# Attention and a squared-ReLU MLP on one core: a third chunk by plain products, and a planner that costs the DMA traffic

## The chip, the cores and the metric

One core of a Trainium2 chip. The metric is the device time of one execution in microseconds (us): the median of 3 runs was 941.05 us (940.84, 941.05 and 945.44). The profile is of one more execution.

## The reference

```python
def _attn_ref(q, k, v):                      # q, k, v: 8 x 8 x 576 x 64
    scores = scale * np.matmul(q, k.transpose(0, 1, 3, 2))
    bias = slopes[:, None, None] * (-np.abs(rel))[None, :, :]
    mask = (rel >= 0) & (rel < 128)
    scores = np.where(mask, scores + bias[None], -1000000000.0)
    attn = np.exp(scores - np.max(scores, axis=-1, keepdims=True))
    attn = attn / (np.sum(attn, axis=-1, keepdims=True) + 1e-09)
    return np.matmul(attn, v)

def _moe_ref(x, w_in, w_out):                # x: 4608 x 512, d_ff 2048
    h = np.maximum(x @ w_in, 0.0)
    return h * h @ w_out

x = attn_out.transpose(0, 2, 1, 3).reshape(4608, 512)
out = _moe_ref(x, w_in, w_out)
```

## The kernel before

The 4608 tokens are nine chunks of 512 (numbered 0 to 8), and d_ff is 16 blocks f of 128. Everything is fp32: each operand of the MLP is split into a high and a low part of a faster type, and each product of blocks is three matmuls (high-high, high-low, low-high).

**The MLP.** The first product of a chunk, x @ w_in, is made in one of two ways. Chunks 0 and 1 take it directly (`gemm1`, line 287): a block f is 12 matmuls of 512 columns; ScalarE then takes the ReLU (line 301), VectorE squares (304), ScalarE rounds the high part (310) and VectorE subtracts for the low part (312). Chunks 2 to 8 take Strassen's scheme: two blocks f are one unit u (8 units in a chunk), and a unit is seven products of 6 matmuls with 256 columns (`product`, line 363) where the plain way needs 24 matmuls of 512 columns. The products read seven forms of x (B11, T1, B21, B22, T2, T3, T4, made once a chunk by `Couple.out`, line 659) and, for four of the seven, sums of weights. Those sums are computed once (`add_weights`, line 343), written to DRAM, and read again for every unit (`load_sum`, line 358; five buffers in turn). `combine` (line 387) adds the products up on VectorE: u1 needs product 6, u3 needs product 5 and u1, c22 needs product 7 and u3; products 2, 3 and 4 go into the banks that s1, u3 and c22 have read, so they wait for these three. The second product (`second`, line 321) adds 12 matmuls of 512 columns for each f, in four steps m of 3; it runs some 8 steps behind. After the 16th f the four sums go out (`copy_out`, line 331, `send_out`, 337): m = 0 and 2 are copied by VectorE, m = 1 and 3 by ScalarE, into two tiles of two halves each; `copy_out` takes a new tile when m is even and otherwise uses the last one taken.

**Attention.** A couple is 512 tokens of a pair of heads; 36 couples in all, four a chunk, each made well before its chunk is due. A *visit* on TensorE (`visit`, line 684) multiplies the weights of the old couple by its values and makes the scores of the new couple. Behind it runs a chain: bias and minimum on VectorE (454), exp on ScalarE (461), sums and reciprocals on VectorE (473, 474), the multiplication by the reciprocals on GpSimd (485), a transpose by blocks on VectorE (533), four writes each of two halves to DRAM (538) and two reads back in another order (543). The next visit needs both reads. A visit comes every two units.

**The order of the work.** Every engine's order is written out. `Line` (line 965) takes steps with an engine, a cost in us, what they come after, and for TensorE the time that its own order gives; due times run backwards from there (`run`), and each engine takes the ready step that is due first. `HANDS` adds 1.5 us after a DMA issue and 0.25 us after TensorE; a read-back is taken as 0.45 us of issue and 2.5 us of landing, whatever else the DMA engines carry. `rest` (line 1033) builds the steps: visits in the direct chunk 1 stand behind the f's of `FIRSTS`, later ones behind every even unit; the sums of weights are all due in chunk 1 (`SUM0` to `SUM3`); the seven products go in the order 1 5 6 7 2 3 4.

## Time and profile before

| | before |
|---|---|
| median of 3 runs | 941.05 us |
| the profiled execution, own time | 940.9 us |
| its span in the profile | 939.1 us |
| mean granted clock of TensorE | 0.987 |
| TensorE busy | 878.9 us (94%) |
| VectorE, ScalarE, GpSimd busy | 680.4, 397.6, 132.6 us |
| DMA | 184.23 MB, 196 GB/s on average |

TensorE's share counts matmuls that overlap one another as busy, so a busy share of 94% does not say that 6% is all there is to gain: what a matmul takes when nothing is late has to be read from stretches in which nothing waits. "Idle before" is time in which an engine stood still, with what ended it. The granted clock is 1.0 at full speed (2.4 GHz) and 0.5 at the lower level (1.2 GHz).

### The profile page before, as it was taken

What the parts mean: (1) busy time and instruction counts of PE and PEld (TensorE: products, weight loads), DVE (VectorE), ACT (ScalarE), POOL (GpSimd) and SP (SyncE); (2) the same over time, 40 slices, a digit from 0 to 9 for tenths busy, and PEclk for the clock granted to TensorE, in tenths of its full rate; (3) what the DMA queues carried; (4) which work ended last, traced back from release to release, by engine and by line L of the source; (5) the groups of instructions that cost most, each with busy time, mean ns of one, the idle gap of its engine ahead of it and who ended that gap; (6) DMA issues with size and microseconds to landing.
All of it is one profiled execution on the core that took longest, in us unless ns stands there. A gap on an engine that the chain in (4) does not pass through costs nothing.

```text
span 939.1 us, 20863 instructions
## 1 busy us (share of the span) xinstructions
PE 878.9 (94%) x7788; PEld 790.8 (84%) x7792; DVE 680.4 (72%) x1952; ACT 397.6 (42%) x1096; POOL 132.6 (14%) x154
## 2 busy tenths in 40 slices
PE   9999999989888999998999998999989999999998
PEld 5788888777788888888888897999888988999997
DVE  7999858998666877776777776677667867755453
ACT  7898754445322433333433342344433343322211
POOL 4322011111011111111011111111111111100000
PEclk9999999999999999999999999999999999999999
DMA  9995454667676647666777677666656776654331
GB/s 347 379 363 160 134 177 138 237 209 236 191 204 177 178 131 243 197 187 175 228 208 203 184 209 220 176 208 198 188 185 195 213 226 188 176 173 147 99 115 46
DMA packets 123909, 184.23 MB, mean 196 GB/s; under 512 B 11808, under 2 KB 55072, under 8 KB 122784
## 3 DMA queue, kind: packets, MB, share of 16 engines
q1 hardware_dynamic: 123376, 182.30, 63.5%
q8 instruction: 62, 1.02, 0.4%
q10 hardware_dynamic: 432, 0.59, 0.2%
q14 instruction: 39, 0.32, 0.1%
HBM read 143.46 MB, written 39.39 MB: 195 GB/s over the span
## 4 chain that ended last, share of the span: by engine, by line
PE 46%; DMA 25%; DVE 16%; ACT 5%; SPq 4%; issue 4%; DVEq 0%; ACTq 0%; POOLq 0%
PE acc L327 21%; DMA pp<-way 14%; PE g L382 7%; PE s L382 5%; DMA way<-pp 4%; PE s L692 4%; SPq L538 3%; PE g L702 3%; PE g L295 3%; DVE pp L533 2%; DMA raw<-in_dram 2%; DMA sum<-sums 2%; DMA out_dram<-o 2%; ACT t L461 2%; DVE r L389 2%
## 5 line engine op out<-in xcount | busy, mean ns | idle before, releaser
L327 PE MATMUL acc<-h,w 128*128 128x512 f32 x1728 | 405.3, 382 | 0.0
L327 PEld LDWEIGHTS acc<-h,w 128*128 128x128 f32 x1728 | 329.1, 197 | 33.4 <-issue 4.6
L485 POOL TENSOR_TENSOR t<-t,nm 128x768 f32<-128x768 f32 x57 | 92.0, 1615 | 193.2 <-DVE nm L474 116.5
L461 ACT ACTIVATE t<-t,nm 128x192 f32<-128x192 f32 x256 | 113.9, 447 | 10.8 <-DVE nm L454 10.7
L454 DVE CUSTOM_DVE_ANT_0 t<-g,cst 128x192 f32<-128x192 f32 (+4 forms) x192 | 53.1, 312 | 87.3 <-PE g L702 85.7
L414 DVE TENSOR_TENSOR h<-r,h 128x512 fp32r<-128x512 f32 x112 | 79.7, 717 | 46.0 <-ACT h L411 44.9
L411 ACT CAST h<-r 128x512 fp32r<-128x512 f32 x112 | 68.5, 617 | 97.4 <-PE acc L327 48.5
L295 PE MATMUL g<-x,w 128*128 128x512 f32 x384 | 89.7, 383 | 6.8 <-ACT r L301 3.0
L382 PEld LDWEIGHTS g<-B,w 128*128 128x128 f32 x672 | 90.0, 191 | 5.6 <-ACT r L301 1.0
L382 PE MATMUL g<-B,w 128*128 128x256 f32 x672 | 93.6, 275 | 0.6 <-ACT r L301 0.6
L692 PE MATMUL s<-pp,v 64*64 64x64 f32 (+1 forms) x1648 | 63.4, 261 | 32.6 <-DMA pp<-way 29.9
L295 PEld LDWEIGHTS g<-x,w 128*128 128x128 f32 x384 | 71.2, 189 | 21.0 <-issue 5.8
L692 PEld LDWEIGHTS s<-pp,v 64*64 64x64 f32 x1648 | 47.7, 143 | 45.8 <-DMA pp<-way 29.3
L382 PE MATMUL s<-T,sum 128*128 128x256 f32 x672 | 84.1, 275 | 0.0
L382 PEld LDWEIGHTS s<-T,sum 128*128 128x128 f32 x672 | 81.6, 192 | 1.2
L406 DVE SCALAR_TENSOR_TENSOR r<-r 128x512 f32<-128x512 f32 x112 | 77.0, 692 | 6.9
L399 ACT ACTIVATE r<-g 128x256 f32<-128x256 f32 x56 | 21.5, 385 | 127.3 <-PE g L382 127.3
L433 POOL MEMSET t<- 64x256 f32 (+1 forms) x56 | 14.2, 253 | 402.3 <-PE g L702 375.8
L389 DVE TENSOR_TENSOR r<-g,u 128x256 f32<-128x256 f32 x112 | 47.3, 422 | 22.7 <-PE g L382 20.7
L382 PE MATMUL g<-B,sum 128*128 128x256 f32 x336 | 50.1, 285 | 12.9 <-DVE r L389 12.9
L533 DVE STREAM_TRANSPOSE pp<-t 128x768 f32<-128x768 f32 x64 | 60.8, 964 | 0.2
L382 PEld LDWEIGHTS g<-B,sum 128*128 128x128 f32 x336 | 41.8, 191 | 19.4 <-DVE r L389 19.4
(108 smaller groups left out, 1118.4 us busy)
## 6 DMA issues: line engine op xcount, KB each, us to landing
sum<-sums SPq DMA_DIRECT2D x224, 256.0 KB, 4.6
pp<-way SPq DMA_DIRECT2D x64, 512.0 KB, 5.6
way<-pp SPq DMA_DIRECT2D x256, 80.0 KB, 2.0
raw<-in_dram SPq DMA_DIRECT2D x32, 512.0 KB, 7.9
qk<-in_dram SPq DMA_DIRECT2D x32, 320.0 KB, 3.1
v<-in_dram SPq DMA_DIRECT2D x32, 320.0 KB, 4.0
qk<-in_dram SPq DMA_DIRECT2D x36, 256.0 KB, 4.0
out_dram<-o SPq DMA_DIRECT2D x35, 256.0 KB, 2.4
```

Of the source, the lines that this page charges most:

```text
L295: nc.tensor.matmul(g, w, in_turn(xs[cc][:, part]), start=i == 0, stop=i == 11)
L327: self.nc.tensor.matmul(self.acc[m], w, in_turn(h), start=(f == 0 and i == 0), stop=(f == NF - 1 and i == 2))
L382: nc.tensor.matmul(to, w, in_turn(t[:, part]), start=i == 0 and k in (1, 5, 6, 7), stop=i == 5, skip_group_check=True,)
L389: V, add = nc.vector, lambda to, a, b: nc.vector.tensor_tensor(to, a, b, op=ALU.add)
L406: V.scalar_tensor_tensor(r, r, 0.0, r, op0=ALU.max, op1=ALU.mult)
L411: nc.scalar.copy(both[:, 0], r)
L414: V.tensor_tensor(hl, r, hh.bitcast(F32), op=ALU.subtract)
L454: self.nc.vector.tensor_tensor_reduce(self.t[r, m, a:e], spot, table[r, a:e], -0.125, least, ALU.add, ALU.min, to,)
L461: e = self.nc.scalar.activation(self.t[:, m], self.t[:, m], AF.Exp, bias=nm[:, m : m + 1], scale=-1.0, accum_out=nm[:, 4 + m : 5 + m],)
L485: self.nc.gpsimd.tensor_tensor(self.t, self.t, rec.unsqueeze(2).to_broadcast([128, 4, 192]), op=ALU.mult)
L533: nc.vector.transpose(squares.rearrange("p b m c -> p m b c"), self.t.rearrange("p m (b c) -> p m b c", c=32))
L692: made.append(mm(to, w, x, start=first and n < 2, stop=not first, skip_group_check=True))
```

## The change

It makes chunk 2 directly, so that three chunks are direct and six go by Strassen's scheme (`NDIR = 3`). The visits behind direct f's become eight (`FIRSTS`), and the sums of weights become due over the two direct chunks 1 and 2. In direct chunks after the first, ScalarE squares. For the third chunk a couple's output is split into two parts (`high`, `low`) where it was seven forms. The order of the seven products is 1 5 6 2 7 3 4, with steps of the second product among them in odd units. Four score matmuls of the new couple (`ahead`) are issued in front of the visit, without a wait for the read-back. `copy_out` takes its tile by m. The planner has one lag for each engine, the DMA transfers of all kinds in turn on one "wire" of 225 KB a us, 1.5 us to spare on read-backs, and steps that share the port of VectorE and GpSimd kept apart.

```diff
+NDIR = 3
+LAGS = {"DVE": 0.13, "Activation": 0.12, "Pool": 0.17, "PE": 0.05}
+WIRE = 225.0
+SPARE = {"rl": 1.5}
+ORDER = ((1, 5, 6, 2, 7, 3, 4), (1, 5, "g", "g", 6, 2, 7, "g", 3, "g", 4))
-FIRSTS = (18, 22, 25, 29)
+FIRSTS = (18, 22, 26, 29, 33, 37, 41, 45)
...
-        if c or f in SQUARES:
+        if c == 0 and f in SQUARES:
...
     def copy_out(self, c, m):
-        if m % 2 == 0:
-            self.both = self.op.tile()
-        self.out_tile[c, m] = self.both[:, m % 2]
+        self.out_tile[c, m] = self.op.all[m // 2][:, m % 2]
...
+def ahead(K, old, new):
+    old.S = K.sc.tile([128, 2, 512], F32, name="s")
+    new.front(old.S, [pool.tile([128, 512], F32, name="g") for pool in (K.low, K.big)])
+    scores(K, new, (0, 0, 0, 1))
...
+    def send(self, name, us, kb, after, do, land, lag):
+        self.add(name, "SP", us, after, do, lag=0.0)
+        self.add(land, "wire", kb / WIRE, [name], None, lag=lag)
...
-                d = min(d, due[n] - TIGHT * us - self.hand(name, self.steps[n][0]))
+                same = s.engine == "PE" and self.steps[n].engine == "PE"
+                d = min(d, due[n] - s.us - (0.0 if same else s.lag) - SPARE.get(name[0], 0.0))
...
-            L.add(("rd", k), "SP", 0.45, [("wl", k), ("wr", 2 * w), ("wr", 2 * w + 1)], step)
-            L.add(("rl", k), f"way{k}", 2.5, [("rd", k)])
+            L.send(("rd", k), 0.4, 512, [("wl", k), ("wr", 2 * w), ("wr", 2 * w + 1)], step, ("rl", k), 1.3)
...
+        if new:
+            first = ("A", v)
+            L.pe(first, 0.3, [*loaded, *banks], do(ahead, K, old, new))
...
+        if c < NDIR:
+            L.add(("x", v, "high"), "Activation", 0.5, [here], do(C.out, "high"))
+            L.add(("x", v, "low"), "DVE", 0.61, [("x", v, "high")], do(C.out, "low"))
...
-            due = L.time + SUM2 + SUM3 * u
-            L.add(("sm", u, i), engine, us, [chain, *after, *more], step, due)
+            L.add(("sm", u, i), engine, us, [chain, *more], step, port=engine == "DVE", due=span[0] + (span[1] - span[0]) * (u + 1) / NPR)
...
-    for n in range(NF, 2 * NF):
+    for n in range(NF, NDIR * NF):
...
-        for what in (1, 5, "g" if u % 2 else None, 6, 7, "g" if u % 2 else None, 2, 3, 4):
+        for what in ORDER[u % 2]:
```

**TensorE, an even unit of a Strassen chunk.** The rows are the last five products (B21 is read by product 2, B22 by 3, T4 by 4, T2 by 6, T3 by 7; two rows each, one for each half of the 256 rows of x's features). Before:

```order
L382 MATMUL s_5492<-T20_0_116,sum1_97 128x256 x3
L382 MATMUL s_5492<-T21_130,sum1_97 128x256 x3
L382 MATMUL s_5492<-T30_0_117,sum2_98 128x256 x3
L382 MATMUL s_5492<-T31_131,sum2_98 128x256 x3
L382 MATMUL g_5475<-B210_0_114,w8_701 128x256 x3
L382 MATMUL g_5475<-B211_128,w8_701 128x256 x3
L382 MATMUL g_5483<-B220_0_115,sum3_99 128x256 x3
L382 MATMUL g_5483<-B221_129,sum3_99 128x256 x3
L382 MATMUL s_5492<-T40_0_118,w9_758 128x256 x3
L382 MATMUL s_5492<-T41_132,w9_758 128x256 x3
```

Now:

```order
L380 MATMUL s_5235<-T20_0_116,sum4_99 128x256 x3
L380 MATMUL s_5235<-T21_130,sum4_99 128x256 x3
L380 MATMUL g_5217<-B210_0_114,w8_699 128x256 x3
L380 MATMUL g_5217<-B211_128,w8_699 128x256 x3
L380 MATMUL s_5235<-T30_0_117,sum0_95 128x256 x3
L380 MATMUL s_5235<-T31_131,sum0_95 128x256 x3
L380 MATMUL g_5225<-B220_0_115,sum1_96 128x256 x3
L380 MATMUL g_5225<-B221_129,sum1_96 128x256 x3
L380 MATMUL s_5235<-T40_0_118,w9_756 128x256 x3
L380 MATMUL s_5235<-T41_132,w9_756 128x256 x3
```

Product 2 has moved between 6 and 7. In the new order products 3, 4 and 7 have a wait for VectorE; before, 3 and 4 had one.

**VectorE, behind the fourth visit of a chunk** (tt holds sums for the forms; u and r2 with L389 or L387 are u1, u3 and c22 of `combine`; STREAM_TRANSPOSE is the transpose in front of the writes). Before:

```order
L473 TENSOR_SCALAR nm_6984<-nm_6984 128x4
L474 RECIPROCAL nm_6984<-nm_6984 128x4
L414 TENSOR_TENSOR h0_88<-r2_92,h0_88 128x512
L665 TENSOR_TENSOR tt_137<-now_138,far11_136 128x256
L473 TENSOR_SCALAR nm_6985<-nm_6985 128x4
L474 RECIPROCAL nm_6985<-nm_6985 128x4
L665 TENSOR_TENSOR tt_137<-tt_137,far11_136 128x256
L533 STREAM_TRANSPOSE pp_7105<-t1_84 128x4x6x32
L389 TENSOR_TENSOR u_93<-s_7096,u_93 128x256
L389 TENSOR_TENSOR r2_92<-g_7070,u_93 128x256
L389 TENSOR_TENSOR r2_92<-s_7096,r2_92 128x256
L533 STREAM_TRANSPOSE pp_7129<-t0_83 128x4x6x32
```

Now:

```order
L471 TENSOR_SCALAR nm_6712<-nm_6712 128x4
L472 RECIPROCAL nm_6712<-nm_6712 128x4
L412 TENSOR_TENSOR h0_88<-r2_92,h0_88 128x512
L471 TENSOR_SCALAR nm_6713<-nm_6713 128x4
L472 RECIPROCAL nm_6713<-nm_6713 128x4
L387 TENSOR_TENSOR u_93<-s_6835,u_93 128x256
L531 STREAM_TRANSPOSE pp_6853<-t1_84 128x4x6x32
L387 TENSOR_TENSOR r2_92<-g_6816,u_93 128x256
L531 STREAM_TRANSPOSE pp_6871<-t0_83 128x4x6x32
L387 TENSOR_TENSOR r2_92<-s_6835,r2_92 128x256
```

The sums for the forms have moved behind the transposes, and the second transpose now stands in front of c22.

**ScalarE, behind the visit in the first unit of a chunk**, where the chunk before goes out (L461 or L459 is exp of one quarter m of a half, L335 or L333 the copies of m = 1 and m = 3). Before:

```order
L461 ACTIVATE t1_84,nm_7270<-t1_84,nm_7270 128x192
L335 COPY o0_86<-acc_6236 128x512
L461 ACTIVATE t1_84,nm_7270<-t1_84,nm_7270 128x192
L335 COPY o0_86<-acc_6238 128x512
L461 ACTIVATE t0_83,nm_7271<-t0_83,nm_7271 128x192 x4
```

Now:

```order
L333 COPY o0_86<-acc_5978 128x512
L683 CAST B110_1_119<-far0_133 128x256
L409 CAST h0_88<-r2_92 128x512
L459 ACTIVATE t0_83,nm_6997<-t0_83,nm_6997 128x192
L389 COPY u_93<-g_7093 128x256
L459 ACTIVATE t0_83,nm_6997<-t0_83,nm_6997 128x192 x3
L333 COPY o3_100<-acc_5980 128x512
```

Before, both copies went into the same half of tile o0, the second of them in front of four exps; now they go into two tiles, and the second copy stands behind the exps.

## Rows read from the trace of the kernel before

**Rows 1.** The page: busy time; DMA issues by line, KB each, us to landing.

```profile
PE 878.9 (94%) x7788; PEld 790.8 (84%) x7792; DVE 680.4 (72%) x1952; ACT 397.6 (42%) x1096; POOL 132.6 (14%) x154
...
pp<-way SPq DMA_DIRECT2D x64, 512.0 KB, 5.6
way<-pp SPq DMA_DIRECT2D x256, 80.0 KB, 2.0
```

**Rows 2.** Windows, one row a stage: stretch, its length, engines' busy time (instructions), clock, DMA.

```profile
131.30:237.10 105.80, 97.62 (x770) 83.25 (x769) 90.18 (x235) 48.31 (x122) 14.44 (x16) 1.00 0.62 200
237.10:348.80 111.70, 99.59 (x925) 92.36 (x926) 75.50 (x242) 37.39 (x116) 14.86 (x16) 0.94 0.63 180
348.80:847.60 498.80, 469.56 (x4558) 432.70 (x4557) 358.32 (x1071) 185.42 (x565) 69.44 (x68) 0.99 0.68 198
847.60:935.20 87.60, 85.69 (x553) 80.08 (x551) 42.16 (x78) 18.24 (x37) 0.00 (x0) 1.00 0.32 96
```

**Rows 3.** Chain in order of time: start, length, what; pieces that wait for nothing.

```profile
99.90 2.59 PE g L295 x12
102.49 2.59 PE acc L327 x12
...
849.07 1.35 PE s L382 x12
```

**Rows 4.** Windows of two visits, from the last matmul before to the first after.

```profile
634.20:636.90 2.70, 2.70 (x97) 2.50 (x96) 0.84 (x4) 0.00 (x0) 0.31 (x1) 1.00 0.43 158
582.00:589.50 7.50, 4.28 (x98) 3.79 (x97) 1.49 (x10) 0.00 (x0) 0.51 (x2) 0.82 0.58 205
```

**Rows 5.** Waits of TensorE in the stretch 131.3 to 237.1: total, times, longest.

```profile
PE g L295 <- DVE nm L454: 2.9, 3, 1.4
PE g L295 <- ACT r L301: 2.3, 3, 0.9
```

**Rows 6.** The same, stretch 348.8 to 847.6.

```profile
PE s L692 <- DMA pp<-way: 19.4, 19, 2.5
PE g L382 <- DVE r L389: 9.0, 23, 0.9
```

**Rows 7.** Timeline, TensorE, an even unit: the second product and the third.

```profile
577.93 0.83 PE L382 MATMUL g<-B,w 128*128 128x256 f32 x6
579.14 0.94 PE L382 MATMUL g<-B,sum 128*128 128x256 f32 x6 [0.38 <-DVE r L389]
```

**Rows 8.** Timeline, VectorE, the same unit: u1 and u3.

```profile
578.20 0.42 DVE L389 TENSOR_TENSOR u<-s,u 128x256 f32<-128x256 f32 x1 [0.80 <-PE s L382]
578.66 0.42 DVE L389 TENSOR_TENSOR r<-g,u 128x256 f32<-128x256 f32 x1
```

**Rows 9.** Timeline, ScalarE, after the visit that ends at 560.5.

```profile
566.79 0.59 ACT L335 COPY o<-acc 128x512 f32<-128x512 f32 x1 [2.31 <-DMA out_dram<-o]
```

**Rows 10.** Timeline, TensorE, where the next visit gets its data.

```profile
585.57 0.68 PE L692 MATMUL s<-pp,v 64*64 64x64 f32 x23 [2.51 <-DMA pp<-way]
```

**Rows 11.** Timeline, TensorE, a stage behind a visit that ends at 636.9.

```profile
636.90 4.16 PE L327 MATMUL acc<-h,w 128*128 128x512 f32 x18
...
658.16 0.79 PE L692 MATMUL s<-pp,v 64*64 64x64 f32 x29 [0.32 <-DMA pp<-way]
```

**Rows 12.** Timeline, GpSimd, the same stage.

```profile
644.51 1.49 POOL L485 TENSOR_TENSOR t<-t,nm 128x768 f32<-128x768 f32 x1 [0.72 <-DVE nm L474]
```

**Rows 13.** Timeline, VectorE, the same stage: the second transpose.

```profile
646.71 0.97 DVE L533 STREAM_TRANSPOSE pp<-t 128x768 f32<-128x768 f32 x1
```

**Rows 14.** Timeline, the DMA queue (SP), the same stage: last writes, last read.

```profile
647.96 1.82 SPq L538 DMA_DIRECT2D way<-pp  x4
...
652.33 0.37 SPq L543 DMA_DIRECT2D pp<-way  x1
```

**Rows 15.** Line 485, the products by the reciprocals on GpSimd.

```profile
L485 POOL TENSOR_TENSOR t<-t,nm x57: 1461/1493/2000, 43.2 to 818.3; 128x768 f32<-128x768 f32 x57
```

## What I expect

> **What bounds the kernel.** I read the page first: TensorE is busy for 878.9 of 939.1 us [rows 1], so the question is what stretches TensorE's own order. The windows by stage [rows 2] cut the span into a head of 131.3 us, which the change leaves as it is; the direct chunk 1 (105.8); Strassen chunk 2 (111.7); chunks 3 to 7 (498.8); chunk 8, which has no visits of its own (87.6); and a tail of 939.1 - 935.2 = 3.9. The chain in order of time gives the pieces as they run when nothing is late [rows 3]: 12 matmuls of a direct block 2.59 us, four steps m of the second product 2.59, two Strassen products 1.35, so 0.67 each. An undisturbed visit takes 2.7, the first of [rows 4]. From these, a direct chunk needs 16 x 5.18 + 4 x 2.7 = 93.7, and two Strassen units with their visit 14 x 0.67 + 16 x 0.648 + 2.7 = 22.4. Measured against that, the direct chunk loses 12.1 us, chunk 2 loses 111.7 - 89.6 = 22.1, and chunks 3 to 7 lose 498.8 - 20 x 22.4 = 50.8, or 2.5 for each of their 20 visits.
>
> The waits of TensorE [rows 6] name the two sources. 19.4 us in chunks 3 to 7 wait for the read-back in front of a visit. A long wait also drops the granted clock: the second stretch of [rows 4] holds 7.50 - 4.28 = 3.2 us of waiting, its clock is 0.82 on average, part of it at 1.2 GHz, and the visit's own work takes 4.28 us where the other takes 2.70, so 1.6 more. And 23 times product 3 waits for u3 on VectorE. That loss is larger than the idle time in the list, because a matmul's end is modelled: product 2 starts at 577.93 and product 3 at 579.14 [rows 7], 1.21 us later where 0.67 would do, so 0.54 is lost. In the direct chunk TensorE waits for VectorE and ScalarE [rows 5], where VectorE is busy for 90.18 of 105.8 us [rows 2].
>
> **Chunk 2 by plain products.** Work: 93.7 instead of 89.6, so 4.1 more. In exchange chunk 2 has no product waits; its forms of x and 32 of the loads of weight sums fall away, work of VectorE, ScalarE and the DMA queue that lies beside TensorE's and that I count as nothing. The losses stay to be estimated. Sums of weights are spread over twice the time and ScalarE takes the squares (it is busy for 48.3 of 105.8 us, so there is room; the work that covers them is four steps m between two blocks). I take 4 us for chunk 1 and 3 for chunk 2, against 12.1 before. Two visits come early: between the f's 26 and 29 lie 3 x 5.18 = 15.5 us, and between the last direct visit and that in the first Strassen unit 12 steps m, two blocks and seven products, 7.8 + 5.2 + 4.7 = 17.7; a read-back takes about 18 to 20 us from visit to visit (next part, less the product work), so I add 2.5 and 0.5. Sum 10 (between 3, if nothing is late, and 24, if both chunks lose what chunk 1 lost): 2 x 93.7 + 10 = 197.4, where the two chunks took 217.5.
>
> **Product order.** u1 starts 578.20 - 577.93 = 0.27 us behind the boundary between two products, lasts 0.42, and product 3 follows 0.06 behind the end of u3 [rows 7, 8]. One VectorE step between two products thus takes 0.75 us. In the new order product 7 waits for u1 and product 4 for c22, each with one product of 0.67 as cover: 0.08 each, and product 3 finds u3 done. An even unit loses 0.16 instead of 0.54. An odd unit, which lost nothing, gains a loss of some 0.16, since its transposes stand ahead of u3 and c22. Two units and a visit: 22.4 + 0.32 = 22.8 (bounds: 22.4 with no loss, 23.8 if c22 comes 1 us late).
>
> **The read-back.** Take the stage behind the visit that ends at 636.9 [rows 11]. The second half's multiplication on GpSimd ends at 646.00 [rows 12], its transpose at 647.68 [rows 13], 10.8 us behind the visit; its writes are issued until 649.78, the second read goes out at 652.33 [rows 14], and the visit gets its data at 658.16, after 0.32 of waiting [rows 11]. In the new order the sums for the forms no longer stand ahead of the second half's reciprocals, and the second transpose stands ahead of c22. GpSimd then follows its first product without a break and ends 0.5 to 0.7 earlier; product 6 is over 3.9 + 1.35 + 1.3 + 0.67 = 7.2 us behind the visit, u1 starts at 7.5, and u1, a transpose, u3 and the other transpose take 0.42 + 0.97 + 0.42 + 0.97, so until 10.3. With 1.82 of issue, 2.0 for a write to land and 5.6 for a read [rows 1], the data is there at 10.3 + 1.8 + 2.0 + 5.6 = 19.7. TensorE comes to the visit after its units at 3.9 + 7.3 + 2.6 + 4.7 + 1.3 + 0.3 of product losses + 0.2 for the score matmuls put ahead = 20.3. The four matmuls themselves are only moved; they wait for the same banks as the visit did. So this stage has no wait by the sum, and I take 0.4 for its spread.
>
> Once a chunk the outputs go out in the chain. In the case of rows 9 the copy of m = 3 waits 2.31 us for a DMA, because both copies of ScalarE had been given the same half of one tile; four exps stand behind it, and the next visit waits 2.51 us for its second half [rows 10]. With the tile taken by m it cannot happen, and the copy stands behind the exps anyway. What is late next there is the second read, queued on SP behind two loads of weight sums that wait for products of the next even unit (the later of them is its third, over at 3.9 + 7.3 + 0.2 + 2.6 + 3 x 0.67 = 16.0 us behind the visit): with the issue 16.2, and 16.2 + 5.6 = 21.8, so 1.5 of waiting. Mean over four visits: (3 x 0.4 + 1.5) / 4 = 0.7, no clock loss in most.
>
> The Trainium skill speaks against these 5.6 us: DMA: Bandwidth & Descriptors, Anatomy of one DMA, fits about 2.0 us plus bytes over 436 GB/s, an estimate of 3.2 us for 512 KB (its fit is for the path through GpSimd; these reads are issued by SP). By the page no read would be late and the 0.7 would be 0; the rows here have 5.6 with other transfers under way, and the measurement decides.
>
> **Sum.** Head 131.3; direct chunks 197.4; chunks 3 to 7 20 x (22.8 + 0.7) = 470.0; chunk 8 87.6 - 4 x (0.54 - 0.32) = 86.7; tail 3.9. Together 889.3. The profiled execution's own time is 940.9 for a span of 939.1, so 1.8 more: 891.1. It stands 0.15 under the median of 941.05, so I say 891.
>
> **Rivals.**
> 1. *Read-backs as late as before.* The transfers, not the order, set their landing: two reads, sums and inputs share the DMA engines, and what is issued earlier only queues earlier. For it: 5.6 us for 512 KB. Against it: in the case of [rows 9, 10] the cause is on ScalarE, and visits such as the first of [rows 4] wait for nothing in the same traffic. Chunks 3 to 7 then keep 2.5 - 0.62 for product 3 = 1.9 a visit: 20 x 1.2 = 24 more, and the direct chunks lose 24 rather than 10: 891 + 38 = 929.
> 2. *VectorE's queue behind the transposes.* The second transpose now waits for GpSimd with c22 behind it, and product 4 waits for c22. GpSimd's step takes 1.49 in the median and up to 2.00 [rows 15]; with that and exps half a microsecond later, product 4 is 1 us late in each of 20 stages: 891 + 20 = 911.
> 3. *No wait left at all.* Reads land soon enough everywhere; then 20 x 0.7 and 3 us in the direct chunks go: 874. It is what the skill's fit above would make of it.
> 4. *The reads held up on SP (slower than before).* The second read is queued behind a load of weight sums, and that load waits for a product that frees its buffer. If this held it in every stage until 16.2 us, as it does once a chunk, and it then took 0.9 more than the median, data would come at 22.7: 2.4 of waiting, and 1.6 of lower clock each time, 4.0 in place of 0.7: 891 + 20 x 3.3 = 957. It decides from 50 / 20 = 2.5 us a visit above my 0.7. Against it: in the other stages the load ahead of the read waits for a product that is over by some 10 us behind the visit.
>
> **Chances and range.** My forecast 0.70, rival 1 0.13, rival 2 0.09, rival 3 0.05, rival 4 0.03. The forecast's own bounds are 878 (half of the waits, 5 us in the direct chunks) and 905 (1.4 a visit); the range goes from 878 to 914, to take in rival 2, and leaves rivals 1, 3 and 4 out. A measurement of this kernel tells a difference of 0.5% (4.7 us). All cases but rival 4 are faster by more than that: faster 0.95, same 0.02, slower 0.03.
>
> **What would show it.** Right: the two direct chunks in about 197 us; chunks 3 to 7 in about 94 each; TensorE's waits for the read-back down by more than half; ScalarE's copies of the output never waiting for a DMA; the clock near 1.0 in every slice; product 3 without a wait and two small ones on products 7 and 4. Wrong: waits for the read-back of over 1 us in most visits; product 4 or 7 waiting 0.5 us or more behind a transpose; a direct stretch much over 200 us with TensorE waiting for ScalarE, which now squares.

## The result, and the profile after

The changed kernel takes 911.1 us (median of 4 runs, 908.4 to 913.6) where the kernel before took 942.2 beside it: a ratio of 0.966, 95% interval 0.963 to 0.970. The forecast was 891 in a range of 878 to 914. The gain is there, but 20 us of the forecast are missing. The profiled execution took 908.4 us for a span of 906.6. Two of the ten executions of one kernel below (two direct chunks) ran in a slower state; its ratio leaves them out, its median does not.

The page of the changed kernel, as in [rows 1] (busy time; clock in 40 slices; DMA issues):

```profile
PE 873.7 (96%) x7648; PEld 782.4 (86%) x7648; DVE 624.3 (69%) x1862; ACT 417.6 (46%) x1114; POOL 129.8 (14%) x154
...
PEclk9999999999999999999999999999999999999999
...
pp<-way SPq DMA_DIRECT2D x64, 512.0 KB, 5.2
way<-pp SPq DMA_DIRECT2D x256, 80.0 KB, 1.9
```

Its windows by stage, as in [rows 2]: the two direct chunks, chunks 3 to 7, chunk 8 (stretch, length, busy time of PE, PEld, DVE, ACT, POOL, clock, DMA):

```profile
130.90:329.00 198.10, 191.92 (x1550) 168.37 (x1549) 125.49 (x390) 104.74 (x256) 29.07 (x32) 0.99 0.55 168
329.00:816.30 487.30, 468.28 (x4558) 431.09 (x4557) 342.97 (x1068) 186.38 (x565) 66.08 (x68) 1.00 0.67 202
816.30:902.70 86.40, 86.37 (x553) 80.61 (x551) 41.75 (x77) 18.20 (x36) 0.00 (x0) 1.00 0.31 97
```

| stage | before | forecast | after |
|---|---|---|---|
| head | 131.3 | 131.3 | 130.9 |
| chunks 1 and 2 | 217.5 | 197.4 | 198.1 |
| chunks 3 to 7 | 498.8 | 470.0 | 487.3 |
| chunk 8 | 87.6 | 86.7 | 86.4 |
| tail | 3.9 | 3.9 | 3.9 |

All that is missing in this execution, 17 us, is in chunks 3 to 7. The waits of TensorE there, as in [rows 6] (engine, line, releaser: us in total, times, longest):

```profile
PE s L712 <- DMA pp<-way: 12.6, 9, 2.4
PE s L380 <- DVE u L387: 3.6, 9, 1.2
PE acc L327 <- DVE T L663: 1.6, 3, 0.5
PE g L380 <- DMA sum<-sums: 0.4, 1, 0.4
```

The wait of product 3 for u3, 9.0 us in [rows 6], is gone. In its place product 7 waits for u1. The read-backs make TensorE wait 9 times instead of 19, in front of 9 of the 20 visits instead of 15. Of their 12.6 us, 9.9 stand in front of five visits: in each chunk the one whose chain runs behind the chunk's end, where the outputs go out too. In the direct chunks, where [rows 5] had VectorE and ScalarE, two visits wait for their data, the one behind f 22 for 2.1 us and the one behind f 29 for 2.8, and hardly anything else is left:

```profile
PE s L712 <- DMA pp<-way: 4.9, 2, 2.8
...
PE g L295 <- ACT r L301: 0.4, 1, 0.4
```

Idle time is not all that is lost (the prediction said so of product 3). So I split chunks 3 to 7 by starts: from the first matmul of each product, step m or visit to that of the next, less 0.67 for a product and 0.648 for a step. What is left over in front of and inside the 20 visits is "visits", all else "products". The work itself is 395 in every kernel (280 products and 320 steps; 394 in the forecast by its rounded 22.4 a pair, and its 470 has 22.72 rounded to 22.8). Each row is one execution, and two executions of one kernel can differ by some us: the second profile of the changed kernel has 490.8 for these chunks.

| chunks 3 to 7, us | products | visits | sum with the work |
|---|---|---|---|
| before | 19.2 | 84.5 | 499 |
| forecast | 6.4 | 68 | 470 |
| changed | 19.0 | 73.3 | 487 |

Nothing was gained at the products as a whole. Products of even units lose some 8 us instead of 13; but products of odd units lose 5 instead of 1.5, and the steps m 5 instead of 3. Part of what product 3 no longer loses is lost in front of and behind product 7. Timeline of TensorE in an even unit, products 6, 2, 7 and 3 (start, length, what), to be set beside [rows 7]:

```profile
597.93 0.83 PE L380 MATMUL s<-T,sum 128*128 128x256 f32 x6
598.60 0.83 PE L380 MATMUL g<-B,w 128*128 128x256 f32 x6
599.28 0.94 PE L380 MATMUL s<-T,sum 128*128 128x256 f32 x6
600.05 0.83 PE L380 MATMUL g<-B,sum 128*128 128x256 f32 x6
```

Product 7 begins on time here and shows no idle time at all; still its six matmuls take 0.94 instead of 0.83, and product 3 begins 0.77 behind it instead of 0.67 (the last section shows where this goes).

Why the five visits behind the chunk ends wait is seen in the stage behind the visit that ends at 629.9. VectorE: u1, u3 and c22 of the odd unit, the first transpose, c12, the second transpose.

```profile
638.78 0.40 DVE L387 TENSOR_TENSOR u<-s,u 128x256 f32<-128x256 f32 x1
639.21 0.42 DVE L387 TENSOR_TENSOR r<-g,u 128x256 f32<-128x256 f32 x1
640.20 0.43 DVE L387 TENSOR_TENSOR r<-s,r 128x256 f32<-128x256 f32 x1 [0.57 <-PE s L380]
640.54 0.97 DVE L531 STREAM_TRANSPOSE pp<-t 128x768 f32<-128x768 f32 x1
641.52 0.42 DVE L387 TENSOR_TENSOR r<-g,u 128x256 f32<-128x256 f32 x1
641.86 0.97 DVE L531 STREAM_TRANSPOSE pp<-t 128x768 f32<-128x768 f32 x1
```

The DMA queue (SP): the eight writes, and the two reads between loads of weight sums:

```profile
641.54 4.47 SPq L536 DMA_DIRECT2D way<-pp  x8
...
646.60 0.38 SPq L541 DMA_DIRECT2D pp<-way  x1
...
648.13 0.37 SPq L541 DMA_DIRECT2D pp<-way  x1
```

And TensorE, where the next visit gets its data:

```profile
654.64 1.10 PE L712 MATMUL s<-pp,v 64*64 64x64 f32 x29 [2.37 <-DMA pp<-way]
```

The second transpose ends 12.9 us behind the visit, the second read goes out at 18.2, the data is used at 24.7. The prediction's sum for a stage in the middle of a chunk had 10.3 for that transpose, a read at 14.1 and the data at 19.7; behind a chunk's end it had the read at 16.2, held up by loads in the queue, and the data at 21.8. Beside the first of these the data is 5.0 us later: 2.6 are on VectorE, 1.5 between the transpose and the read, on the DMA queue, and 0.9 in the read itself, which takes 6.5 us here where the prediction had 5.6.

### The profile page after: what moved, and what is told of

The parts are those of the page before. It is cut to its first block, busy times and chain, and to the rows that moved or that the text cites. A ratio compares the mean times of both kernels' runs of the same rounds, so it can differ in the third digit from the quotient of the medians.

```text
span 906.6 us, 20533 instructions
## 1 busy us (share of the span) xinstructions
PE 873.7 (96%) x7648; PEld 782.4 (86%) x7648; DVE 624.3 (69%) x1862; ACT 417.6 (46%) x1114; POOL 129.8 (14%) x154
## 3 DMA queue, kind: packets, MB, share of 16 engines
q1 hardware_dynamic: 118768, 173.91, 61.7%
## 4 chain that ended last, share of the span: by engine, by line
PE 65%; DMA 17%; DVE 7%; ACT 6%; issue 3%; SPq 2%; DVEq 0%; ACTq 0%; POOLq 0%
PE acc L327 31%; DMA pp<-way 9%; PE g L295 9%; PE g L380 9%; PE s L380 7%; PE s L712 4%; DMA raw<-in_dram 3%; PE g L692 2%; DMA way<-pp 2%; ACT t L459 2%; DMA sum<-sums 1%; SPq L536 1%; PE s L692 1%; DMA qk<-in_dram 1%; DVE pp L531 1%
## 5 line engine op out<-in xcount | busy, mean ns | idle before, releaser
L295 PE MATMUL g<-x,w 128*128 128x512 f32 x576 | 133.3, 381 | 2.4 <-ACT r L301 1.2
L295 PEld LDWEIGHTS g<-x,w 128*128 128x128 f32 x576 | 107.9, 189 | 20.1 <-ACT r L301 2.9
L409 ACT CAST h<-r 128x512 fp32r<-128x512 f32 x96 | 59.7, 622 | 134.3 <-PE acc L327 73.2
L459 ACT ACTIVATE t<-t,nm 128x192 f32<-128x192 f32 x256 | 114.6, 450 | 9.5 <-DVE nm L452 8.8
L412 DVE TENSOR_TENSOR h<-r,h 128x512 fp32r<-128x512 f32 x96 | 68.0, 708 | 53.1 <-ACT h L409 52.4
L380 PEld LDWEIGHTS s<-T,sum 128*128 128x128 f32 x576 | 73.5, 191 | 9.5 <-DVE u L387 5.3
L380 PE MATMUL g<-B,w 128*128 128x256 f32 x576 | 80.0, 275 | 0.1
L380 PEld LDWEIGHTS g<-B,w 128*128 128x128 f32 x576 | 75.6, 191 | 2.5 <-ACT u L389 0.3
L404 DVE SCALAR_TENSOR_TENSOR r<-r 128x512 f32<-128x512 f32 x96 | 65.5, 689 | 4.8 <-DVE r L387 0.9
L312 DVE TENSOR_TENSOR h<-r,h 128x512 fp32r<-128x512 f32 x48 | 36.0, 751 | 26.4 <-ACT h L310 26.1
L301 ACT ACTIVATE r<-g 128x512 f32<-128x512 f32 x48 | 28.5, 595 | 53.3 <-PE g L295 41.8
L459 ACT ACTIVATION_READ_ACCUMULATOR t<-t,nm 128x1 f32 x256 | 48.8, 191 | 0.0
```

The costliest lines, as they stand in the source:

```text
L295: nc.tensor.matmul(g, w, in_turn(xs[cc][:, part]), start=i == 0, stop=i == 11)
L312: nc.vector.tensor_tensor(hl, r, hh.bitcast(F32), op=ALU.subtract)
L380: nc.tensor.matmul(to, w, in_turn(t[:, part]), start=i == 0 and k in (1, 5, 6, 7), stop=i == 5, skip_group_check=True,)
L404: V.scalar_tensor_tensor(r, r, 0.0, r, op0=ALU.max, op1=ALU.mult)
L409: nc.scalar.copy(both[:, 0], r)
L412: V.tensor_tensor(hl, r, hh.bitcast(F32), op=ALU.subtract)
```

## Experiments

My theory at the start was that the missing time sits in the small waits that the new order puts in front of products. Rivals: the products are slower whatever they wait for; the waits only move on; the late read-backs are the cause. One table of the changed kernel and all twelve runs; the kernel before, timed beside them, took 938.7 to 942.6. The ratios are to be compared, more than the times; the last two columns are of one execution each.

| kernel | us | ratio to before, 95% | chunks 3 to 7 | waits there for read-backs |
|---|---|---|---|---|
| changed | 911.1 | 0.966 (0.963 to 0.970) | 487.3 | 12.6 |
| changed, again | 912.0 | 0.969 (0.963 to 0.975) | 490.8 | 15.0 |
| old order, both units | 898.9 | 0.952 (0.947 to 0.956) | 480.0 | 3.5 |
| old order, even units | 909.8 | 0.968 (0.963 to 0.972) | 486.1 | 9.2 |
| old order, odd units | 894.3 | 0.951 (0.947 to 0.955) | 474.2 | 3.0 |
| earlier transposes | 902.3 | 0.956 (0.952 to 0.959) | 478.8 | 1.6 |
| two tiles | 914.9 | 0.968 (0.962 to 0.973) | 494.8 | 19.2 |
| two tiles, old order | 891.3 | 0.944 (0.940 to 0.947) | 469.9 | 6.7 |
| the same, read-backs due earlier | 886.9 | 0.944 (0.940 to 0.948) | 469.7 | 6.9 |
| two direct chunks | 926.2 | 0.984 (0.981 to 0.987) | 489.5 | 14.7 |
| planner without wire | 905.3 | 0.968 (0.963 to 0.972) | 479.9 | 10.7 |
| no scores ahead | 906.1 | 0.968 (0.965 to 0.970) | 481.3 | 8.0 |
| before, copies apart | 935.9 | 0.996 (0.993 to 0.999) | 492.2 | 14.9 |

**The order of the seven, undone.**

```diff
-ORDER = ((1, 5, 6, 2, 7, 3, 4), (1, 5, "g", "g", 6, 2, 7, "g", 3, "g", 4))
+ORDER = ((1, 5, 6, 7, 2, 3, 4), (1, 5, "g", "g", 6, 7, "g", "g", 2, 3, 4))
```

> The changed kernel with the order of the seven products of before. The prediction's step says that an even unit then loses 0.54 instead of 0.16 and an odd one nothing instead of 0.16: 0.22 more a pair, 24 x 0.22 = 5 us more: 916. My theory from the two traces (the losses in front of products are 0.69 a pair before and 0.52 after, since each wait that was put in costs some 0.1 more than its idle time): 0.1 a pair, 2 to 3 us more: 913. Rival (the new order is worth nothing or costs): 911 or less.

It took 898.9, 12 us less than the changed kernel. The prediction's step and my theory both fall: each had this kernel slower. By the same split, products lose 23.3 (4 us more, so the products do gain from the new order) and visits 61.7 (12 less), each from one execution. The waits of TensorE in its chunks 3 to 7:

```profile
PE g L380 <- DVE r L387: 9.7, 21, 1.9
PE s L712 <- DMA pp<-way: 3.5, 4, 2.4
```

So product 3 waits for u3 again, and the read-backs hardly matter. The next three runs ask why an order of products makes read-backs late.

**The old order in even units alone.**

```diff
-ORDER = ((1, 5, 6, 2, 7, 3, 4), (1, 5, "g", "g", 6, 2, 7, "g", 3, "g", 4))
+ORDER = ((1, 5, 6, 7, 2, 3, 4), (1, 5, "g", "g", 6, 2, 7, "g", 3, "g", 4))
```

> The changed kernel with the order of before in even units alone; odd units keep the new one. The planner then writes VectorE's steps behind a chunk's end as in the changed kernel (u1, u3 and c22 ahead of both transposes), while TensorE's products in the unit that follows a visit's chain are as before. My theory (the new order costs 12 us mostly because the second transpose of the stage behind a chunk's end, and with it the second read-back, comes some 1 to 2 us later on VectorE, not because of the products themselves): the visits behind a chunk's end keep their waits of about 2 us, and the time stays within 4 of the changed kernel, 907 to 912. Rival (the order of the products in even units costs TensorE the 12 us): 899, as with the old order in both. Second rival (it is the odd units' products): 911 as well, but then without waits of 2 us in the visits behind a chunk's end.

909.8: no gain, as my theory had it. The five visits behind chunk ends wait 0.6 to 1.4 us each, 6.0 in all, less than the 2 I expected of each, in a chunk that the waits for u3 make longer. Its waits in chunks 3 to 7:

```profile
PE s L712 <- DMA pp<-way: 9.2, 8, 1.6
PE g L380 <- DVE r L387: 6.6, 19, 0.4
```

**The old order in odd units alone.**

```diff
-ORDER = ((1, 5, 6, 2, 7, 3, 4), (1, 5, "g", "g", 6, 2, 7, "g", 3, "g", 4))
+ORDER = ((1, 5, 6, 2, 7, 3, 4), (1, 5, "g", "g", 6, 7, "g", "g", 2, 3, 4))
```

> The changed kernel with the order of before in odd units alone; even units keep the new one. The chain behind a visit runs beside an odd unit, so its order sets when u3 is due, and the planner's VectorE order behind a chunk's end becomes that of the kernel with the old order in both: both transposes ahead of c22. My theory (what the new order costs is the late transposes, set by product 3 standing one step m nearer in odd units): the waits of about 2 us behind chunk ends go, and the time is that of the old order in both, 899, or up to 3 less, since even units lose 0.4 instead of 0.6 a pair. Rival (the two halves of the order each cost some of the 12 us): 903 to 907.

894.3, at a ratio of 0.951 beside 0.952 with the old order in both: all of the gain is in the odd units. That even units give another 3 us on top can't be told from these ratios. Its waits in chunks 3 to 7, and VectorE in the stage that answers to the one shown above (u1, first transpose, u3, second transpose, c22):

```profile
PE g L380 <- DVE r L387: 3.2, 2, 1.9
PE s L712 <- DMA pp<-way: 3.0, 3, 1.7
```

```profile
633.03 0.42 DVE L387 TENSOR_TENSOR u<-s,u 128x256 f32<-128x256 f32 x1
633.36 0.97 DVE L531 STREAM_TRANSPOSE pp<-t 128x768 f32<-128x768 f32 x1
634.25 0.39 DVE L387 TENSOR_TENSOR r<-g,u 128x256 f32<-128x256 f32 x1
634.56 0.96 DVE L531 STREAM_TRANSPOSE pp<-t 128x768 f32<-128x768 f32 x1
635.44 0.38 DVE L387 TENSOR_TENSOR r<-s,r 128x256 f32<-128x256 f32 x1
```

The visit ends at 624.4 there, so the second transpose ends 11.1 us behind it instead of 12.9; over the five stages behind chunk ends it ends 10.7 to 11.5 us behind the visit, where the changed kernel has 11.5 to 12.9. The five visits there wait 0.2 us in all instead of 9.9. The cause is in the planner: due times run backwards from TensorE's order. In odd units the new order has three steps m in front of product 3 where the old one had four, so u3 is due 0.65 us earlier. The planner's code, worked through for this stage, has u3 due 1.35 us ahead of the transposes in the changed kernel and 0.70 here. With that, the low part of the unit before (line 412), which u3 needs, comes ahead of the first half's reciprocals: behind a chunk's end, where two output copies make VectorE late, these start 6.7 us behind the visit instead of 5.9, and u1, u3 and c22 come ahead of both transposes. There c22 also holds VectorE 0.57 us for product 7 (shown above) while the first transpose, whose input was ready at 638.6, stands behind it. The plan does not see this lateness: it has the second transpose end 11.3 us behind this visit with either order.

**Earlier transposes, the new order kept.**

```diff
-SPARE = {"rl": 1.5}
+SPARE = {"rl": 3.5}
```

> The changed kernel with the read-backs due 3.5 us before their visit instead of 1.5, which puts both transposes of the stage behind a chunk's end ahead of the output copies and of c22 on VectorE. My theory: 9.9 of the 12.6 us that TensorE waits for read-backs in chunks 3 to 7 stand in front of the five visits behind a chunk's end, and there the second transpose is what is late; it ends some 3 us earlier, these waits fall to 2 us or less in all: 8 us less, 903. Rival (the transfers set the landing, not the transpose): the waits stay, 911. Second rival: c22 and the output copies come later and product 4 or the next chunk's first product waits by as much as is gained: 909 to 913.

902.3, as the theory had it, and the waits for read-backs are nearly gone. But the second rival is there as well: product 3 waits for u3, now in odd units, and products and steps m lose 25.9 instead of 19.0. Its waits in chunks 3 to 7:

```profile
PE g L380 <- DVE r L387: 5.4, 16, 0.5
...
PE s L712 <- DMA pp<-way: 1.6, 4, 0.6
```

**Two tiles for `s`.** u1 reads the first bank of `s`, product 7 writes the second; both lay in one tile, and the wait was set for the tile.

```diff
-            S = self.sc.tile([128, 2, 512], F32, name="s")
-            self.bank_b, self.bank_d = S[:, 0, 0:256], S[:, 1, 0:256]
+            self.bank_b, self.bank_d = (t[:, 0:256] for t in self.apart())
...
+    def apart(self):
+        return [pool.tile([128, 512], F32, name="s") for pool in (self.sc, self.sd)]
...
```

> The changed kernel with the two banks of `s` as two tiles instead of one tile over both; product 6 writes the one, product 7 the other. In the changed kernel product 7's first matmul waits for the VectorE step u1, though u1 reads the first bank and product 7 writes the second: both stand in one tile. The copy of a couple's output by ScalarE becomes two instructions. My theory (the loss in chunks 3 to 7 that I put at 0.32 a pair of units sits in small waits in front of products, about 1.04): the wait on u1 goes, and with it the 0.16 and 0.18 us lost between products 2 and 7 in even and odd units of the changed kernel's trace; 24 pairs of units times 0.33 = 8 us less: 903. First rival (the loss is in the products themselves, whose matmuls follow each other more slowly after any change of weights): no change, 911. Second rival (the wait only moves on to product 3 or 4, which wait for u3 and c22 in the same VectorE queue): 909 to 911, with the losses in front of products 3 and 4 up by what is gained in front of product 7.

The wait on u1 is gone, and the products lose 12.6 instead of 19.0: the first half of my theory holds. Yet the time is 914.9, and the ratio (0.968 beside 0.966) can't be told from the one before the edit. The wait did not move to product 3 or 4, as a rival had it, but to the visits. Waits in chunks 3 to 7, then windows of two visits (stretch, length, busy time, clock), as in [rows 4]:

```profile
PE s L717 <- DMA pp<-way: 19.2, 13, 3.3
PE g L382 <- DMA sum<-sums: 2.0, 4, 0.9
```

```profile
656.23:663.74 7.51, 4.75 (x105) 4.20 (x105) 0.85 (x6) 0.00 (x0) 0.31 (x1) 0.77 0.52 198
632.96:635.77 2.81, 2.81 (x105) 2.63 (x104) 0.82 (x4) 0.00 (x0) 0.31 (x1) 1.00 0.85 311
```

TensorE comes to the visit sooner, and the chain from visit to visit over VectorE and the DMA queue does not. The wait grows by what the products gave up, and the first of the two visits also runs part of its time at 1.2 GHz (0.77 on average) and does the same work in 4.75 us instead of 2.81. While read-backs are late, this saving at the products is worth nothing.

**Two tiles with the old order.** Both edits above (in the kernels with two tiles, u1 is no longer planned behind product 7).

> As the kernel with two tiles, and with the order of the seven products of before (1 5 6 7 2 3 4). There the wait of u1 for product 7, which came from the shared tile, does not arise: u1 may run beside product 7, u3 beside product 2 and c22 beside product 3, each with more work between it and the product that waits for it than in the new order. My theory: no product waits in either unit, so the two-tile kernel's remaining losses in front of products 3 and 4 go too, some 0.2 to 0.3 a pair, 24 x 0.25 = 6 us below the kernel with two tiles: 897. Rival (the order of the seven matters by itself, as the prediction had it: product 3 stands two products behind 6 and waits for u3): 0.5 lost in every even unit, 48 half-units, 24 x 0.5 = 12 us above the kernel with two tiles: 915.

891.3, with the products at 10.7 and the visits at 64.0: 6 us under my number and far from the rival's 915. With the transposes early, most of what the products give up does arrive: 12.6 us by the split against the old order with one tile, and 7.6 in the time (898.9 to 891.3). The waits in chunks 3 to 7 are these:

```profile
PE s L717 <- DMA pp<-way: 6.7, 7, 1.4
PE g L382 <- DVE r L389: 3.2, 2, 1.9
```

**The same, read-backs due 2.5 us ahead** (`SPARE = {"rl": 2.5}`).

> As the kernel with two tiles and the old order, and with the read-backs due 2.5 us ahead of their visit instead of 1.5. Behind a chunk's end both reciprocals and the first transpose then stand ahead of u3, the second ahead of c22; other stages hardly change. My theory: the visits of chunks 3 to 7 in the kernel with two tiles and the old order lose 20 x (3.12 - 2.7) = 8.4 us to read-backs, half of it behind chunk ends; this half goes and the rest stays: 4 us less, 887. Rival (u3 comes late behind the transposes and product 3 waits for it, as in the kernel with earlier transposes): 891 or more.

886.9, which is the expected number, but not by the expected way: the waits for read-backs are 6.9 where they were 6.7, chunks 3 to 7 take 469.7 where they took 469.9, and the ratio is the same (0.944 both times). It can't be told from the kernel without this edit. These two are the fastest I ran, some 20 us under the changed kernel.

**Two direct chunks again.**

```diff
-NDIR = 3
+NDIR = 2
-FIRSTS = (18, 22, 26, 29, 33, 37, 41, 45)
+FIRSTS = (18, 22, 25, 29)
...
```

The lines left out, among others, move the parts of x to other places of memory and let the first sum of weights wait for the copies of chunk 0's output.

> The changed kernel with two direct chunks again: chunk 2 by Strassen's scheme, the sums of weights within chunk 1, everything else as changed. My theory (the 19.4 us that chunks 1 and 2 gained, 217.5 to 198.1, come from making chunk 2 directly with the sums spread over two chunks): chunk 1 takes 105.8 again and chunk 2 its 111.7 less the 2.3 a chunk by which chunks 3 to 7 became shorter: 911 + 17 = 928. Rival (the planner gained them, and the third direct chunk is worth little: a Strassen chunk takes the 97.5 of chunks 3 to 7, and chunk 1 loses 7 us to the crowded sums, 105.8): 97.5 + 105.8 = 203, so 911 + 5 = 916.

926.2, near my 928, but by other parts. Chunks 1 and 2 take 114.1 + 101.1 = 215.2, against 198.1; I had expected 105.8 and 109, which is the same sum. The loss is in chunk 1, where ScalarE now squares and the sums of weights are crowded again; which of the two it is was not separated. Windows of both chunks, and the waits in chunk 1:

```profile
130.90:245.00 114.10, 101.33 (x769) 87.52 (x768) 80.56 (x223) 58.07 (x138) 14.06 (x16) 0.93 0.59 188
245.00:346.10 101.10, 95.10 (x925) 87.97 (x924) 71.64 (x240) 36.67 (x115) 13.75 (x16) 0.98 0.65 198
```

```profile
PE g L298 <- ACT r L304: 11.3, 2, 8.2
```

**The planner without its wire.**

```diff
-WIRE = 225.0
-SPARE = {"rl": 1.5}
+OLD = {"og": 3.5, "wl": 0.4, "rl": 2.5, "lql": 2.5, "lvl": 2.5, "sml": 4.0, "Sl": 2.3}
+SPARE = {}
...
-        self.add(land, "wire", kb / WIRE, [name], None, lag=lag)
+        self.add(land, f"wire{land}", OLD[land[0]], [name], None, lag=0.0)
```

> The changed kernel with the planner's old rule for transfers: every landing costs a fixed time on a channel of its own (2.5 us for a read-back, 4.0 for a sum's way out) and no spare time ahead of a read-back. My theory (the early read-backs of chunks 3 to 7 come from the wire and the spare time, which put the second transpose ahead of c22 and of the sums for the forms): the waits for read-backs in chunks 3 to 7 rise from 12.6 us by 8 to 10 and some visits lose clock: 922. Rival (they come from the tile for the output copy and from the longer stage, the planner's rule being without effect): 911, within 2.

No rise: 905.3, and by the ratio not to be told from the changed kernel. My theory of it falls. The direct chunks lose 3.5 us, chunks 3 to 7 take 7.4 less in this execution:

```profile
130.90:332.55 201.65, 193.62 (x1548) 169.76 (x1548) 124.60 (x387) 104.21 (x256) 27.81 (x32) 0.98 0.52 163
332.55:812.41 479.86, 465.54 (x4557) 428.94 (x4556) 341.34 (x1071) 185.72 (x565) 65.55 (x68) 1.00 0.68 206
```

This run also shows that the late transpose is not the whole of the waits behind chunk ends. Its second transposes there are as late as in the changed kernel (11.9 to 12.8 us behind the visit, beside 11.5 to 12.9), and yet the five visits wait 3.9 us in all instead of 9.9. The two reads stand side by side in its DMA queue, without loads of weight sums between them: in the mean of the five stages the second read goes out 0.9 us earlier and takes 5.4 us instead of 6.2. Here is the queue behind the visit that ends at 630.7, to be set beside the one above:

```profile
646.18 1.70 SPq L541 DMA_DIRECT2D pp<-way  x2
```

**The four score matmuls back in the visit** (`ahead` is taken out, and its step in the planner).

> The changed kernel with the four score matmuls back inside the visit. My theory: they are worth their own time, some 0.3 us, in the visits that wait for a read-back (12 of 28 in the changed kernel's trace): 12 x 0.3 = 3.6 us, so 914 to 915. Rival (the wait is longer than what is put ahead anyway, and the planner's order in between changes more than these matmuls do): within 2 of 911 or below it.

906.1, the rival's side; by the ratio (0.968) again no difference. Here too VectorE's order in between changes, so what the four matmuls alone are worth was not isolated.

**The kernel before with the copies apart.**

```diff
-        if m % 2 == 0:
-            self.both = self.op.tile()
-        self.out_tile[c, m] = self.both[:, m % 2]
+        self.out_tile[c, m] = self.op.all[m // 2][:, m % 2]
```

> The kernel before with one edit: the copy of output m takes its half of its own tile, so that ScalarE's second copy no longer waits for the first one's transfer. My theory: the two worst visits behind a chunk's end (waits of 3.22 and 2.58 us, at a lower clock) lose their wait, 6 us in all: 936 to 937. Rival (all that chunks 3 to 7 gained, 11.5 us, is this): 931. Second rival (the second read is late there anyway): 941 to 942.

935.9 beside 940.2: 4 us, ratio 0.993 to 0.999. Chunks 3 to 7 go from 498.8 to 492.2, and their waits for read-backs from 19.4 [rows 6] to this:

```profile
PE s L690 <- DMA pp<-way: 14.9, 13, 2.5
```

That is near my 6 in size, but not by the way I gave: the two worst visits still wait 2.53 and 2.07 us where it was 3.22 and 2.58, because the second read is late there anyway (the second rival), and the rest comes from smaller losses. The 6.6 us in chunks 3 to 7 are about half of what these gained in the changed kernel.

**The changed kernel again.**

> The changed kernel itself, once more, beside the others on one chip. All theories: 911 within 3, a ratio of 0.966; it tells how far the times of the other runs, made on other chips, may be compared with 911.

912.0 and 0.969: the times of the other runs may be set beside 911. The five visits behind chunk ends wait here too, 12.2 us in all.

## Why the prediction came out as it did

**Chunk 2 by plain products: right.** 198.1 where the sum said 197.4, and undoing it costs 17 us in its two chunks. Of the two early visits that the prediction named, the one behind f 29 waits 2.8 us where it had added 2.5, the one in the first Strassen unit 0.3 where it had added 0.5; the visit behind f 22, which it had not named, waits 2.1, and less than expected is lost elsewhere.

**Product order: the mis-sized term.** The prediction took 0.32 us a pair, 0.08 for each wait with a product as cover. The trace has 0.95 a pair (19.0 / 20), with no gain on the kernel before (19.2). An even unit's products lose some 0.4 us instead of 0.16, an odd unit's 0.24 instead of 0.16, and the steps m, which the term left out, 5 us in all (3 before). The price of 0.08 was too low for one reason that the trace shows: a product that finds its operand just in time still loses 0.1, in its own matmuls or in front of the next. This is 12.6 of the 17 us. Half of the term rested on a wait that only the shared tile made.

**The read-back: right in size for most stages, wrong about what the order does.** 12.6 us of idle time over 20 visits are 0.63 each, against 0.7, and 73.3 against 68 with what surrounds them; but that is down by a third from 19.4, where the prediction had named a fall by more than half as a sign of being right. And the step "in the new order ... the second transpose stands ahead of c22" was read off a stage in the middle of a chunk. Behind chunk ends the new order puts it behind c22; I looked there at the SP queue alone and found 1.5 us, where it is 2.0, late on VectorE first and then on the queue. And where the transposes came early, it was not the order that did it: with the old order in odd units they are early too, and the kernel is 17 us faster. The change would have reached about 894 without its new order for odd units.

**The terms are not additive.** The sum treated the products and the read-back as terms of their own. Two tiles in the new order show that they are not: in the two profiled executions the products gave 6.4 us and the visits took back 13.9, and by the ratio nothing was gained. Nor do the runs account for the whole gain of 31 us: the third direct chunk is worth 17 and the copies apart 4, the planner's wire and spare time nothing that they can show, and the new order for odd units costs 17. What gave the rest was not isolated.

**The rivals.** VectorE's queue behind the transposes (rival 2) gave the right time, 911, by another mechanism: it had product 4 late by 1 us, and product 4 waits for nothing in the list. The truth was the opposite queue, transposes behind the products' steps. That 911 lies in the stated range is luck to that extent: the forecast's own bounds ended at 905, and the range went on to 914 for rival 2 alone. Rival 1 did not come as stated: the reads land in 5.2 us instead of 5.6 in the median, and the waits went down. But in the five stages behind chunk ends the second read takes 5.9 to 6.5 us, and without the wire these waits fall with the transposes as late, so the transfers have their part in them. Rival 3, no wait left, is what the Trainium skill's fit (DMA: Bandwidth & Descriptors, Anatomy of one DMA) would make of it with its estimate of 3.2 us for a read; the trace has 5.2, and the measurement decides. Rival 4 did not come: no load holds the queue for microseconds in the stage shown, the second read goes out 18.2 us behind the visit, 0.5 behind the landing of its last write.

## What to carry to other kernels

Where a planner runs due times backwards from one engine's order, moving a step of that engine by 0.65 us can turn the order of another, and each kind of stage has to be looked at: the stage that decides is the one with extra work in it, not the usual one. Where a chain from one visit to the next bounds a stage, as here, time saved beside that chain comes back as waiting, and the longer wait costs clock as well (0.77 above); so shorten the chain first, then the rest. A wait between two instructions that share a tile and no data is worth a second tile once the chain is out of the way: 0 in the new order here, 7.6 us in the old one.

## What the runs showed of the hardware that I had not expected

A VectorE instruction on 128 x 4 values takes 0.14 to 1.44 us, by what GpSimd does meanwhile: all 17 of the 54 below that take over 0.3 us run beside a product of GpSimd (line 483) and end 0.02 to 0.03 us behind it. Line 471 in the changed kernel (min, median and max in ns):

```profile
L471 DVE TENSOR_SCALAR nm<-nm x54: 138/168/1436, 155.6 to 786.2; 128x4 f32<-128x4 f32 x54
```

In the stage shown above it is the reciprocals' first step of the second half, and beside it GpSimd multiplies the first half:

```profile
637.21 1.44 DVE L471 TENSOR_SCALAR nm<-nm 128x4 f32<-128x4 f32 x1
```

```profile
637.16 1.47 POOL L483 TENSOR_TENSOR t<-t,nm 128x768 f32<-128x768 f32 x1 [7.83 <-DVE nm L472]
639.00 1.47 POOL L483 TENSOR_TENSOR t<-t,nm 128x768 f32<-128x768 f32 x1 [0.38 <-DVE nm L472]
```

Both end at 638.6, and GpSimd's second product cannot begin before 639.0. The planner's code keeps such steps apart in its plan (steps marked `port`), and on the chip these two met all the same; my sum for the chain did not allow for it, and had GpSimd go on without a break.

The other is the price of a wait that the list of TensorE's matmuls does not have: a product whose operand comes just in time takes 0.94 us for six matmuls instead of 0.83. The rows of weight loads show where it goes. Below are u1, then the loads for product 2 and for product 7 of the even unit shown above:

```profile
598.80 0.42 DVE L387 TENSOR_TENSOR u<-s,u 128x256 f32<-128x256 f32 x1
```

```profile
598.49 0.75 PEld L380 LDWEIGHTS g<-B,w 128*128 128x128 f32 x6
599.27 0.74 PEld L380 LDWEIGHTS s<-T,sum 128*128 128x128 f32 x6
```

Product 2's first load starts 0.11 us ahead of its first matmul (598.60). Product 7's starts 0.05 behind the end of u1 and together with the first matmul, and the second matmul follows 0.21 behind the first instead of 0.11. In chunks 3 to 7 the first matmul of a product is stretched in this way 60 times, 6.1 us in all, and 27 times, 2.7 us, in the kernel before.
